# Reordering the first units of a fused attention and gated-MLP kernel, new row layouts for two inputs, and another layout of the fallback branch

## Chip, cores and metric

One core of a Trainium2 chip runs the whole program. The metric is the device time of one execution in microseconds (us), median of several executions. The engines are PE (TensorE, matmuls), DVE (VectorE), ACT (ScalarE), POOL (GpSimd) and SP, which here only issues DMAs; PSUM holds what PE writes. All executions reported here are in the undisturbed ("fast") state.

## The reference, cut to what matters

```python
mod = silu(c) @ w_mod                      # six rows of 512: sa, ca, ga, sb, cb, gb
h = layernorm(x) * (1 + ca) + sa           # x: 2048 x 512
q = (h @ wq)                               # 32 heads of 128; 8 groups share k and v
x = x + ga * (softmax(q k^T / sqrt(128)) v) @ wo
h = layernorm(x) * (1 + cb) + sb
z = gelu(h @ w_in);  z1, z2 = halves of z;  z2 = layernorm(z2)
x = x + gb * ((z1 * (w_sp @ z2 + b_sp)) @ w_out)
```

## The kernel before

The attention is a software pipeline of 128 units (8 groups of k and v, 16 query tiles each). A unit has 8 slots. In a slot the kernel first runs what is entered under `at(unit, slot, ...)`, then two score matmuls and an exp of this unit (`qk`), eight value matmuls of the unit before (`pv`), and then the `fill` matmuls, most of them query projections for later units. All engines take this order as their own program order, so an entry in the wrong slot holds up what stands behind it on its engine.

```python
def qk(u, i):
    s_ps = bank2()                                  # one of two PSUM buffers
    for h in range(2):
        nc.tensor.matmul(s_ps[...], lhsT=kT[...], rhs=qTs[b][:, :, ...])     # all four heads of qT
    nc.scalar.activation(out=pTs[u][...], in_=s_ps[...], func=Exp)

def qproj(b, heads, c0, n):                         # a list of matmuls; the fourth of a head copies it
    ...
    nc.vector.tensor_copy(out=qTs[b][...], in_=ps[0][...])                   # L894 in the profiles
```

LayerNorm of the input works in chunks of four tiles. `ln1_stats` is four pairs of statistics on VectorE (DVE), then two small GpSimd (POOL) steps for rstd, the reciprocal of the standard deviation; `ln1_norm` writes xn; `ln1_turn` transposes on TensorE (PE) and modulates on DVE; `ln1_dma` transposes by DMA instead, and `ln1_dma_mod` modulates what has landed, again on DVE.

```python
at(0, 3, lambda: ln1_turn(1, CT - 1, rest0["xn"]))          # rest of chunk 0
for k, fn in enumerate(rest_q):                             # its 16 query matmuls
    fill.setdefault((0, 5 + min(k // 5, 2)), []).append(fn)
ln1_at(1, (0, 7), (1, 3), (1, 6))                           # chunk, slots of stats, norm, turn or modulation
ln1_at(2, (1, 7), (2, 2), (3, 5))
ln1_at(3, (4, 1), (4, 5), (5, 5))
at(2, 5, lambda: nc.gpsimd.dma_start(out=wmod_b, ...))      # 2 MB
at(5, 5, lambda: nc.gpsimd.dma_start(out=win_sb, ...))      # 1.8 MB
...                                                         # v, wo, wq of the next group: slots (5,3), (6,3), (7,3)
```

Ahead of unit 0, the order of the first loads and the idle matmuls that keep PE busy while they are under way:

```python
nc.sync.dma_start(out=c_bf[:], in_=c_dram)                     # c, 1 KB
nc.sync.dma_start(out=x_sb[:, 0, :], in_=x_dram[:, 0, :])      # first tile of x
nc.sync.dma_start(out=wmod_a[:], in_=wmod_dram[:, :, 0:2 * D]) # 1 MB
...
warm(18)                                                       # matmuls on zeros
xns0 = ln1_norm(0, 1, ln1_stats(0, 1))
mod_columns(0, wmod_a, 0)                                      # 32 matmuls, need w_mod
```

At the end every engine reads a flag. If some softmax sum was out of range, a slow general path computes everything again; with these inputs it never runs.

```python
redo = nc.values_load(flag[0:1, 0:1], min_val=0, max_val=P)
with tc.If(redo != 0, preferred_fallthrough_block=False):
    general_path(...)
```

Of the kernel before, what the change touches and what calls it, by code (L numbers as in the profile page):

```python
# [15 lines left out]
P = 128  # L16
# [559 lines left out]
def kernel(  # L576
# [23 lines left out]
    REP = HQ // HKV  # L600
# [5 lines left out]
    NDT = D // P  # L606
# [3 lines left out]
    CT = 512 // P  # L610
# [12 lines left out]
    HK = SK // 2  # L623
    k_rows = A_k_cache[0, 0, 0:HK].rearrange("(p t) d -> p t d", p=P)
    v_rows = A_v_cache[0, 0, 0:HK].rearrange("(p t) d -> p t d", p=P)
    wmod_dram = w_mod.rearrange("(dt p) n -> p dt n", p=P)
    c_dram = c[0].rearrange("(j p) -> p j", p=P)
    win_dram = B_w_in.rearrange("(dt p) f -> p dt f", p=P)
    wout_dram = B_w_out.rearrange("(ft p) d -> p ft d", p=P)

# [32 lines left out]
    def bank(name):  # L663
        return psum.tile([P, 512], FP32, name=name)

    def bank2():
        return psum.tile([P, 1024], FP32, name="s_ps")
# [93 lines left out]

    def warm(n):

        w_ps = bank2()
        for k in range(n):
            nc.tensor.matmul(
                w_ps[:, 0:512].rearrange("p (r d) -> p r d", r=REP),
                lhsT=zeros[:, 0, :],
                rhs=zeros[:],
                start=True,  # L770
                stop=True,
            )
# [23 lines left out]
    def ln1_stats(j0, n):  # L796
        for j in range(j0, j0 + n):
            ln_stats(mv1, j, x_sb[:, j, :])
        return rstd_of(mv1[:, j0 : j0 + n, :], n, "ln1")

    def ln1_norm(j0, n, rstd):
        xns = []
        for j in range(j0, j0 + n):
            xn = res.tile([P, D], BF16, name="xn1", bufs=4)
            normalise(xn[:], x_sb[:, j, :], mv1[:, j, 0:1], rstd[:, j - j0 : j - j0 + 1])
            xns.append(xn)
        return xns

    def hT_of(ch):
        if ch not in hTs:  # L810
            hTs[ch] = res.tile([P, NDT, 512], BF16, name="hT", bufs=NCH)
        return hTs[ch]

    def ln1_mod(dst, src, dt):
        nc.vector.tensor_scalar(
            out=dst,
            in0=src,
            scalar1=modc[:, NDT + dt : NDT + dt + 1],
            scalar2=modc[:, dt : dt + 1],
            op0=ALU.mult,  # L820
            op1=ALU.add,
        )

    def ln1_turn(j0, n, xns, on_act=()):

        ch, c0 = j0 // CT, (j0 % CT) * P
        hT = hT_of(ch)
        for half in range(2):
            t_ps = bank("misc")[:].bitcast(BF16).rearrange("p (k q) -> p k q", k=2)
            for k in range(2):  # L830
                dt = half * 2 + k
                for jj in range(n):
                    nc.tensor.transpose(
                        t_ps[:, k, jj * P : (jj + 1) * P],
                        xns[jj][:, dt * P : (dt + 1) * P],
                        ident[:],
                    )
            for k in range(2):
                dt = half * 2 + k
                dst, src = hT[:, dt, c0 : c0 + n * P], t_ps[:, k, 0 : n * P]  # L840
                if dt in on_act:
                    nc.scalar.activation(
                        out=dst,
                        in_=src,
                        func=ACT.Identity,
                        scale=modc[:, NDT + dt : NDT + dt + 1],
                        bias=modc[:, dt : dt + 1],
                    )
                else:
                    ln1_mod(dst, src, dt)  # L850

    def ln1_dma(j0, n, xns):
        hT = hT_of(j0 // CT)
        for jj in range(n):
            nc.sync.dma_start_transpose(out=hT[:, :, jj * P : (jj + 1) * P], in_=xns[jj][:])

    def ln1_dma_mod(ch):
        for dt in range(NDT):
            ln1_mod(hTs[ch][:, dt, :], hTs[ch][:, dt, :], dt)

    warm(18)
    xns0 = ln1_norm(0, 1, ln1_stats(0, 1))
    mod_columns(0, wmod_a, 0)
    ln1_turn(0, 1, xns0, on_act=(1, 3))
    k_ps = bank("o_ps")[:].bitcast(BF16)
    for kt in range(NKT // 2):
        nc.tensor.transpose(
            k_ps[:, kt * P : (kt + 1) * P], k_nat[:, kt * P : (kt + 1) * P], ident[:]
        )
    nc.scalar.copy(out=kT0[:, 0:HK], in_=k_ps)  # L870
    warm(3)

    def qproj(b, heads, c0, n):

        g, ch = divmod(b, NCH)
        if b not in qTs:
            qTs[b] = early.tile([P, REP, 512], BF16, name="qT")
        one = n * len(heads) <= 512
        ps = {}

        def mm(hh, dt):
            if dt == 0 and (not one or hh == heads[0]):
                ps[0] = bank("misc")
            o0 = (hh - heads[0]) * n if one else 0
            nc.tensor.matmul(  # L885
                ps[0][:, o0 : o0 + n],
                lhsT=wqs[g][:, dt, hh * DH : (hh + 1) * DH],
                rhs=hTs[ch][:, dt, c0 : c0 + n],
                start=(dt == 0),
                stop=(dt == NDT - 1),  # L890
            )
            if dt == NDT - 1 and (not one or hh == heads[-1]):
                hs = heads if one else [hh]
                nc.vector.tensor_copy(  # L894
                    out=qTs[b][:, hs[0] : hs[-1] + 1, c0 : c0 + n],
                    in_=ps[0][:, 0 : len(hs) * n].rearrange("p (h q) -> p h q", q=n),
                )

        return [lambda hh=hh, dt=dt: mm(hh, dt) for hh in heads for dt in range(NDT)]
# [3 lines left out]
    rest0 = {}  # L903
# [7 lines left out]
    def at(it, slot, fn):  # L911
        later.setdefault((it, slot), []).append(fn)
# [149 lines left out]

    fill = {}
    rest_q = qproj(0, list(range(REP)), P, 512 - P)
    at(0, 3, lambda: ln1_turn(1, CT - 1, rest0["xn"]))
    for k, fn in enumerate(rest_q):
        fill.setdefault((0, 5 + min(k // 5, 2)), []).append(fn)

    def ln1_at(ch, stats, norm, turn):
        st = {}  # L1070
        at(*stats, lambda: st.update(r=ln1_stats(ch * CT, CT)))
        at(*norm, lambda: st.update(x=ln1_norm(ch * CT, CT, st["r"])))
        if ch == 1:
            at(*turn, lambda: ln1_turn(ch * CT, CT, st["x"]))
        else:
            at(norm[0], norm[1] + 1, lambda: ln1_dma(ch * CT, CT, st["x"]))
            at(*turn, lambda: ln1_dma_mod(ch))

    ln1_at(1, (0, 7), (1, 3), (1, 6))
    ln1_at(2, (1, 7), (2, 2), (3, 5))  # L1080
    ln1_at(3, (4, 1), (4, 5), (5, 5))
    rest_w = {}
    at(2, 5, lambda: nc.gpsimd.dma_start(out=wmod_b, in_=wmod_dram[:, :, 2 * D : NMOD]))
    at(5, 5, lambda: nc.gpsimd.dma_start(out=win_sb[:], in_=win_dram))
# [5 lines left out]
    def set_fill(b):  # L1090

        fs = qproj(b, list(range(REP)), 0, 512)
        for k, fn in enumerate(fs):
            it, slot = ((b - 1) * CT + k // NDT, k % NDT) if b > 1 else (2 + k // 8, k % 8)
            fill.setdefault((it, slot), []).append(fn)

    def wsp0():
# [5 lines left out]
    for g in range(1, HKV):  # L1103
        it = (g - 1) * NT + 4
# [91 lines left out]
    for it in range(NU + 6):  # L1196
        if it < NU:
            if it % CT == 0 and it // CT + 1 < NB:
                set_fill(it // CT + 1)
        elif it == NU:  # L1200
            free_a.close()
            z2p = fast.enter_context(tc.tile_pool(name="z2p", bufs=1))
            zs["z2"] = z2p.tile([P, NT, FH], BF16, name="z2")
# [154 lines left out]
    fast.close()  # L1358

    redo = nc.values_load(flag[0:1, 0:1], min_val=0, max_val=P)  # L1360
    with tc.If(redo != 0, preferred_fallthrough_block=False):
        general_path(
            tc, A_x, A_k_cache, A_v_cache, A_wq, A_wo, B_x, B_w_in, B_w_sp, B_b_sp, B_w_out,
            c, w_mod, out,
        )
# [30 lines left out]
```

## Time and profile before

| | before |
|---|---|
| median of the first 3 executions | 1338.97 us (1338.56 to 1339.24) |
| span of the profiled execution | 1337.6 us |
| PE busy, PE idle | 1305.1 us, 32.5 us |
| start of unit 0, unit 1, unit 8 | 11.77, 26.98, 92.24 us |
| a unit in steady state | 8.81 us |
| last DVE instruction to the end of the span | 8.3 us |

From unit 8 on nothing is touched by the change until the branch at the end, so three stretches can move: the 11.8 us ahead of unit 0, units 0 to 7, and the tail. The start is a chain through one load (view of the chain that ended last: start us, us, what):

```profile
1.79 5.61 DMA wmod_a<-in_w_mod_dram
7.39 0.05 issue
7.44 0.97 PE misc L782 x32
```

PE's first useful work (L782) waits for w_mod to land at 7.4 us, 5.61 us after its issue.

### The profile page before, as it was taken

To read this page: it belongs to the slowest core of one execution; us is meant where nothing else is said; L and a number is where in the kernel's file an instruction comes from. 1 tells how busy PE (TensorE), PEld (TensorE's weight loads), DVE (VectorE), ACT (ScalarE), POOL (GpSimd) and SP (SyncE) were. 2 spreads that over 40 slices of the span, in tenths; PEclk is the share of its full clock that TensorE was granted. 3 is DMA by queue.
4 is the path that set the end of the run, shared out by engine and by line. 5 is a ranking of instruction groups with operands and counts; after the bars stand their busy time and mean duration, and the time that the engine had idled before them with its cause. 6 is when DMAs were issued, how large, how long until landed. Compare 5 with 4: busy or idle time off the path is not lost.

```text
span 1337.6 us, 27647 instructions
## 1 busy us (share of the span) xinstructions
PE 1305.1 (98%) x12126; PEld 859.4 (64%) x12333; DVE 473.1 (35%) x1163; ACT 1079.3 (81%) x1060; POOL 48.6 (4%) x90
## 2 busy tenths in 40 slices
PE   7999999999999999999999999999999999999996
PEld 3666666666666666666666666666666667644444
DVE  4632222222222222222222222222222566783443
ACT  4898999999999999999999999999999999650000
POOL 1200000000000000000000000000000000020000
PEclk8999999999999999999999999999999999999999
DMA  5541022101311121012110310122101111154200
GB/s 158 131 111 17 14 63 37 21 17 33 64 21 21 33 64 21 17 36 65 17 21 17 74 30 14 21 65 36 21 13 21 25 33 33 29 123 82 55 21 27
DMA packets 146368, 57.59 MB, mean 43 GB/s; under 512 B 136544, under 2 KB 141792, under 8 KB 146240
## 3 DMA queue, kind: packets, MB, share of 16 engines
q1 hardware_dynamic: 141888, 39.29, 15.7%
q0 software_dynamic: 4208, 16.39, 4.1%
q8 instruction: 98, 1.61, 0.5%
q14 instruction: 30, 0.25, 0.1%
q10 hardware_dynamic: 144, 0.07, 0.0%
HBM read 21.37 MB, written 2.10 MB: 18 GB/s over the span
## 4 chain that ended last, share of the span: by engine, by line
PE 94%; SPq 2%; DVE 1%; issue 1%; DMA 1%; POOL 0%; ACT 0%; DVEq 0%
PE s_ps L922 35%; PE o_ps L944 35%; PE misc L885 7%; PE misc L976 6%; PE misc L1273 6%; PE s_ps L1119 2%; PE s_ps L1158 2%; SPq L1056 1%; PE o_ps L1294 1%; PE s_ps L1294 0%; DMA wmod_a<-in_w_mod_dram 0%; DMA hT<-xn 0%; DVE bnst L691 0%; DVE qT L894 0%; DMA out_dram<-yout 0%
## 5 line engine op out<-in xcount | busy, mean ns | idle before, releaser
L929 ACT ACTIVATE pT<-s_ps 128x1024 bf16<-128x1024 f32 x1024 | 1045.9, 1024 | 92.2 <-PE s_ps L922 17.1
L944 PEld LDWEIGHTS <-pT 128*128 128x128 bf16 x8192 | 549.3, 98 | 242.4 <-issue 1.8
L944 PE MATMUL o_ps<-v,pT 128*128 128x129 bf16 x8192 | 632.4, 220 | 0.4 <-DVE onorm L956 0.4
L922 PE MATMUL s_ps<-qT,kT 128*128 128x512 bf16 x2048 | 610.6, 380 | 15.5 <-DVE qT L894 4.7
L955 DVE RECIPROCAL rall<-o_ps 128x2 f32<-128x2 f32 x256 | 43.7, 171 | 742.6 <-PE o_ps L944 742.4
L922 PEld LDWEIGHTS <-kT 128*128 128x128 bf16 x2048 | 199.6, 98 | 126.2 <-DVE qT L894 4.8
L885 PE MATMUL misc<-hT,wq_g 128*128 128x512 bf16 (+2 forms) x462 | 167.7, 373 | 0.0
L976 PE MATMUL misc<-wo_g,oT 128*128 128x512 bf16 x388 | 147.0, 379 | 0.0
L956 DVE TENSOR_TENSOR onorm<-o_ps,rall 128x256 bf16<-128x256 f32 x256 | 108.7, 425 | 9.0 <-DVE rall L955 0.3
L1273 PE MATMUL misc<-wsp,z 128*128 128x512 bf16 (+2 forms) x555 | 100.5, 336 | 1.7 <-DVE gb L1288 1.1
L894 DVE CAST qT<-misc 128x512 bf16<-128x512 f32 (+1 forms) x129 | 87.2, 677 | 4.7 <-PE misc L885 4.7
L1273 PEld LDWEIGHTS <-z 128*128 128x128 bf16 x560 | 50.7, 98 | 49.5 <-issue 1.0
L989 DVE TENSOR_TENSOR xacc<-misc,xacc 128x512 f32<-128x512 f32 x112 | 76.2, 680 | 0.0
L885 PEld LDWEIGHTS <-wq_g 128*128 128x128 bf16 x528 | 51.3, 98 | 2.2 <-issue 1.1
L976 PEld LDWEIGHTS <-oT 128*128 128x128 bf16 x512 | 50.1, 98 | 0.7
L1288 DVE TENSOR_TENSOR gb<-misc,bsp_bc 128x512 bf16<-128x512 f32 (+1 forms) x28 | 18.4, 658 | 53.1 <-PE misc L1273 53.1
L712 POOL MEMSET v<- 128x128 bf16 x8 | 1.6, 204 | 715.9 <-issue 606.9
L1119 PE MATMUL s_ps<-win_sb,hT 128*128 128x448 bf16 x128 | 27.0, 352 | 0.1
L1129 ACT ACTIVATE z<-s_ps 128x896 bf16<-128x896 f32 x16 | 14.7, 917 | 14.9 <-PE s_ps L1119 14.9
L1158 PE MATMUL s_ps<-hT,win_sb 128*128 128x512 bf16 x109 | 24.3, 379 | 0.2
L1166 ACT ACTIVATE z1T<-s_ps 128x1024 bf16<-128x1024 f32 x14 | 14.3, 1024 | 10.0 <-PE s_ps L1158 9.1
L691 DVE BATCH_NORM_STATS2 bnst<-x_sb 128x6 f32<-128x512 bf16 x32 | 21.8, 682 | 0.5
(78 smaller groups left out, 281.2 us busy)
## 6 DMA issues: line engine op xcount, KB each, us to landing
v<-in_A_v_cache_dram POOLq DMA_DIRECT2D x7, 512.0 KB, 6.6
wo_g<-in_A_wo_dram POOLq DMA_DIRECT2D x7, 512.0 KB, 4.8
wq_g<-in_A_wq_dram POOLq DMA_DIRECT2D x7, 512.0 KB, 6.0
oT<-onorm SPq DMA_TRANSPOSE x128, 2.4
wsp<-in_w_mod_dram POOLq DMA_DIRECT2D x1, 2048.0 KB, 9.2
out_dram<-yout SPq DMA_DIRECT2D x15, 128.0 KB, 1.7
win_sb<-in_B_w_in_dram POOLq DMA_DIRECT2D x1, 1792.0 KB, 9.8
x_sb<-in_A_x_dram SPq DMA_DIRECT2D x3, 512.0 KB, 5.7
```

The lines of the kernel that those rows point to most:

```text
L885: nc.tensor.matmul(ps[0][:, o0 : o0 + n], lhsT=wqs[g][:, dt, hh * DH : (hh + 1) * DH], rhs=hTs[ch][:, dt, c0 : c0 + n], start=(dt == 0), s ...
L894: nc.vector.tensor_copy(out=qTs[b][:, hs[0] : hs[-1] + 1, c0 : c0 + n], in_=ps[0][:, 0 : len(hs) * n].rearrange("p (h q) -> p h q", q=n),)
L922: nc.tensor.matmul(s_ps[:, h * 512 : (h + 1) * 512].rearrange("p (r q) -> p r q", r=REP), lhsT=groups[g]["kT"][:, kt * P : (kt + 1) * P], ...
L929: nc.scalar.activation(out=pTs[u][:, 2 * i : 2 * i + 2, :], in_=s_ps[:].rearrange("p (k q) -> p k q", k=2), func=ACT.Exp, scale=inv_sqrt_dh,)
L944: nc.tensor.matmul(o_ps[:, hh % 2, 0 : DH + 1], lhsT=pTs[u][:, kt, hh * P : (hh + 1) * P], rhs=groups[g]["v1"][:, kt, 0 : DH + 1], start=( ...
L955: nc.vector.reciprocal(out=rall[:, c0 : c0 + 2], in_=o_ps[:, :, DH])
L956: nc.vector.tensor_tensor(out=onorms[u][:, hh - 1 : hh + 1, :], in0=o_ps[:, :, 0:DH], in1=rall[:, c0 : c0 + 2].unsqueeze(2).to_broadcast([ ...
L976: nc.tensor.matmul(X_ps[:], lhsT=oTs[u][:, hh, :], rhs=groups[g]["wo"][:, hh, :], start=(hh == 0), stop=(hh == REP - 1),)
L989: nc.vector.tensor_tensor(out=xaccs[j][:], in0=X_ps[:], in1=xaccs[j][:], op=ALU.add)
L1119: nc.tensor.matmul(ps[0][:, hf * 512 : hf * 512 + FC], lhsT=h2Ts[j // CT][:, dt, (j % CT) * P : (j % CT + 1) * P], rhs=win_sb[:, dt, FH + ...
L1158: nc.tensor.matmul(ps[0][:, k * 512 : (k + 1) * 512], lhsT=win_sb[:, dt, f * P : (f + 1) * P], rhs=h2Ts[2 * ch2 + k][:, dt, :], start=(dt ...
L1273: nc.tensor.matmul(g_ps[:, :n], lhsT=z2[:, st, f * P : (f + 1) * P], rhs=wsp[t][:, st, c0 : c0 + n], start=(st == 0), stop=(st == NT - 1 a ...
```

## The change

The intent: let no query copy stand behind LN statistics on DVE, let no score matmul stand behind transposes that still wait, give DMA transposes more time, keep PE busy in unit 0 with four idle matmuls (now on another PSUM bank), read c and w_mod so that a partition's rows are neighbours, and leave the branch layout to the compiler.

```diff
-    wmod_dram = w_mod.rearrange("(dt p) n -> p dt n", p=P)
-    c_dram = c[0].rearrange("(j p) -> p j", p=P)
+    wmod_dram = w_mod.rearrange("(p dt) n -> p dt n", p=P)
+    c_dram = c[0].rearrange("(p j) -> p j", p=P)
...  # in warm(n)
-        w_ps = bank2()
+        w_ps = bank("o_ps")
...
-    at(0, 3, lambda: ln1_turn(1, CT - 1, rest0["xn"]))
+    at(0, 4, lambda: ln1_turn(1, CT - 1, rest0["xn"]))
     for k, fn in enumerate(rest_q):
-        fill.setdefault((0, 5 + min(k // 5, 2)), []).append(fn)
+        fill.setdefault((0, 5 + k // 6), []).append(fn)
+    for i in range(4):
+        fill[0, i] = [lambda: warm(1)]
...
-    ln1_at(1, (0, 7), (1, 3), (1, 6))
-    ln1_at(2, (1, 7), (2, 2), (3, 5))
-    ln1_at(3, (4, 1), (4, 5), (5, 5))
+    ln1_at(1, (1, 0), (1, 5), (1, 7))
+    ln1_at(2, (2, 4), (3, 1), (4, 5))
+    ln1_at(3, (5, 1), (5, 5), (6, 6))
...  # in set_fill(b): unit and slot of the query matmul k of group of tiles b
-            it, slot = ((b - 1) * CT + k // NDT, k % NDT) if b > 1 else (2 + k // 8, k % 8)
+            it, slot = (b - 1) * CT + k // NDT, k % NDT
+            if b == 1:
+                it, slot = 2 + (2 + k) // 16, (1 + k // 2) % 8
+            elif b == 2:
+                it, slot = (5, k // 2) if k < 8 else (it, slot)
...
-    with tc.If(redo != 0, preferred_fallthrough_block=False):
+    with tc.If(redo != 0):
```

More of the change, by code (lines that the diff above doesn't have):

```diff
@@ L762, in warm @@
     def warm(n):
-        w_ps = bank2()
+        w_ps = bank("o_ps")
         for k in range(n):
             nc.tensor.matmul(
-                w_ps[:, 0:512].rearrange("p (r d) -> p r d", r=REP),
+                w_ps[:].rearrange("p (r d) -> p r d", r=REP),
                 lhsT=zeros[:, 0, :],
```

## The prediction

> **What bounds the kernel now.** I read the busy table first, then the waits of PE, then the chain of work over the first 42 us, then busy time by stretch, last the sources of the branch. The page's first part says that PE is the bound, and that little can be won:
>
> ```profile
> PE 1305.1 (98%) x12126; PEld 859.4 (64%) x12333; DVE 473.1 (35%) x1163; ACT 1079.3 (81%) x1060; POOL 48.6 (4%) x90
> ```
>
> PE is idle for 1337.6 - 1305.1 = 32.5 us in all. The attention runs in 128 units of 8 slots (score matmuls L922, exp on ACT, value matmuls L944). In the trace a unit in steady state takes 8.81 us from its first score matmul to the next unit's: 8 slots of 1.10 us, of which 0.885 is the slot's own work and 0.215 one extra matmul. The first units take 15.21, 9.64, 8.81, 10.88, 8.82, 8.81, 9.49 and 8.81 us (they start at 11.77, 26.98, 36.62, 45.43, 56.31, 65.13, 73.94, 83.43; unit 8 at 92.24). So the change can act on units 0 to 7, on the 11.77 us ahead of them, and on the tail. The waits of PE (waiter, releaser: total us, times, longest) name the holes:
>
> ```profile
> PE s_ps L922 <- DVE qT L894: 4.7, 3, 3.0
> PE misc L833 <- DVE xn L680: 1.9, 1, 1.9
> ```
>
> PE waits for the query copy (L894) and for the normalised tile (L680). The chain that ended last, early part (start, us, what), says why:
>
> ```profile
> 14.53 0.90 POOL rstd_ln L676
> 15.45 1.07 DVE xn L680 x3
> 16.52 0.05 issue
> 16.57 0.73 PE misc L833 x10
> ...
> 22.26 0.56 DVE qT L894
> 22.82 0.61 DVE bnst L691
> ...
> 26.02 0.92 DVE qT L894 x2
> 26.98 0.60 PE s_ps L922 x2
> ```
>
> The last two query copies were due at about 22.8 and stand on DVE behind four LN statistics (22.73 to 26.02), because these are put into slot (0,7) ahead of the fills. Before that, the transposes of slot (0,3) wait in PE's order for xn, so that score matmuls which need no xn wait too. Busy time by stretch (length, PE, PEld, DVE, ACT, POOL, then clock, DMA, GB/s):
>
> ```profile
> 16.00:18.00 2.00, 1.81 (x15) 1.03 (x16) 1.51 (x5) 0.17 (x1) 0.00 (x0) 0.89 1.10 348
> 18.00:20.00 2.00, 1.74 (x5) 0.56 (x4) 0.64 (x2) 1.81 (x3) 0.00 (x0) 0.50 0.76 236
> 20.00:22.00 2.00, 2.00 (x10) 1.04 (x9) 0.56 (x1) 1.20 (x2) 0.00 (x0) 0.76 0.00 0
> 24.00:26.00 2.00, 0.00 (x0) 0.00 (x0) 1.90 (x7) 0.04 (x1) 0.00 (x0) 1.00 0.00 0
> 28.00:30.00 2.00, 2.00 (x13) 1.27 (x11) 0.88 (x3) 1.60 (x2) 0.00 (x0) 0.50 0.01 4
> ```
>
> The clock falls to half after each hole; "busy" PE at 0.50 does half the work.
>
> **What the Trainium skill says.** "TensorE: Matmul & The Clock Gate", section "The HAM clock gate", has a free-running window of about 3.4 us after which an idle PE is throttled to half. The trace agrees: 0.89, 0.50, 0.76 over three times 2 us is 0.44 + 2.00 + 0.96 = 3.4 us at half. The same page, on engine queue depths, has ACT and DVE as strict FIFO; the copies behind the statistics show it. "DMA: Bandwidth & Descriptors", "Specifications", sets 512 B as the least piece for full rate. c is read in 2 B pieces, 512 of them: 1 KB lands no sooner than 128 KB.
>
> ```profile
> x_sb<-in_A_x_dram SPq DMA_DIRECT2D x1, 128.0 KB, 2.7
> c_bf<-in_c_dram SPq DMA_DIRECT2D x1, 1.0 KB, 2.8
> ```
>
> "Runtime: NRT & Kernel Launch", "Instruction fetch mechanics", says that a taken branch to a far target stalls for a fetch. The tail agrees (source view of the branch and of the end: ns min/median/max, first to last start):
>
> ```profile
> L1361 PEldq COMPARE_BRANCH  x2: 90/1858/3627, 1327.8 to 1328.1; - x2
> L1361 SPq COMPARE_BRANCH  x2: 38/48/57, 1329.0 to 1332.2; - x2
> L1391 SPq EVENT_SEMAPHORE  x14: 17/28/28, 1336.0 to 1337.6; - x14
> ```
>
> One of PE's branches takes 3.63 us, and SP does nothing visible from its last branch (1332.2) to 1336.0; the span ends 1.6 us later.
>
> **Part by part.**
>
> *c and w_mod by partition.* c becomes 128 pieces of 8 B. In the trace the 512 pieces occupy the queues from 1.88 to 3.13 us, so a quarter takes about 0.3 and 0.9 is saved there. w_mod keeps its 2 KB pieces; its gain is that c and x no longer stand ahead of it: its first piece can't start before its own issue allows (1.79 plus the 1.15 that c's first piece took from issue, 2.94 against 3.10 for the first now, up to some 0.5 later on other engines). It lands now at 1.79 + 5.6 = 7.4, and its 32 matmuls start at 7.43, the start of the path. I take **0.4 us**. wq and the first half of K queue behind it and move along.
>
> *Unit 0.* With old times: exps are 1.02 us, so the first four run 12.40 to 16.5 without a break, as slot (0,3) no longer waits. xn is ready at 16.52 as now; transposes to 17.30, score matmul of slot 4 to 17.73, exp 4 at 17.9 (now 18.90, after the delayed exp 3). hT is complete at 18.63 as now. The 16 query matmuls of 0.16 us go 6, 6, 4: to 19.2, 20.6, 21.6. The last copy (0.56) ends near 22.3, with no statistics before it, and unit 1 starts at about 22.35 in place of 26.98: **4.6 us**. The four idle matmuls cost 4 x 0.215 where PE waits for ACT anyway: nothing. They fill 0.64 of each 1.02 us, which should keep the clock up.
>
> *Unit 1.* It has little extra PE work, so it is bound by ACT, 8 x 1.02 = 8.2, plus some 0.3 for the 16 transposes moved to its last slot: 8.5 against 9.64, since the cold stretch after 27.8 is gone: **1.1 us**.
>
> *Units 2 and 3.* Now 8.81 + 10.88 = 19.69; the extra matmuls (16 query, 4 output projection) stay, so the work is 16 x 0.885 + 20 x 0.215 = 18.5. The 1.2 over it come from DVE waiting for the transposed hT of chunk 2, which competes with the 2 MB of w_mod. The modulation now comes about 11 slots after the transfer instead of 10, and both start later: I count 0.5 of wait at most, hidden by the two PSUM buffers. **1.2 us**.
>
> *Units 4 to 7.* Now 35.93 for 32 x 0.885 + 32 x 0.215 = 35.2. Unit 4 loses its fills, so it has 7.9 us of PE work under 8.2 of ACT: up to 0.25 lost. Chunk 3's transfer still meets the burst of v, win, wo and wq, which POOL issues right after the rstd of this chunk:
>
> ```profile
> DVE hT L815 <- DMA hT<-xn: 9.1, 2, 6.6
> ```
>
> The 6.6 is that wait; it cost PE only 0.4 to 0.7. From rstd to landing are 15.8 us now and the modulation gets one slot more; I expect 5.5 us of DVE wait and again some 0.5 of PE. **0**.
>
> *Branch.* On SP the eight waits for the output stores stand between its two branches, and the fetch comes after the last of them. If the default puts the fallback inline, the far jump comes at 1329.0 and its fetch (3.7) overlaps the stores (until 1331.9): about 3 us. If the automatic choice is the same as now: 0. I can't tell which; half and half, **1.5 us**.
>
> Sum: 0.4 + 4.6 + 1.1 + 1.2 + 0 = 7.3, plus 1.5 is 8.8; less 0.4 for the rivals below: 1338.97 - 8.4 = 1330.5.
>
> **Rivals.** (1) The clock falls anyway. From 14.2 to 17.6 PE has some 2.2 us of work in my schedule, against 1.8 now, which was judged idle; if that isn't enough, 3.4 us run at half and 0.5 to 1.5 come back; then about 1332. (2) DVE becomes the wait in other places: the four statistics at (2,4), 3.2 us, now delay a query copy of chunk 1, and the one at (2,7) needs its PSUM bank; or hT of chunk 3 comes so late that units 6 and 7 lose 2 us. For it speaks the 6.6 us wait, against it that PE rides 6 to 7 slots on two banks; again about 1332. (3) The start is bound by wq, which lands at 9.6 just ahead of the first query matmuls at 9.9, and not by c: only the 0.4 goes. (4) The branch is neutral: 1332; with the full overlap: 1329.
>
> **Range and chances.** Early part 6 to 8.5, branch 0 to 3.5: 1327 to 1333, widened to 1334 for clock and transfers. A gain over 2% would be 26.8 us, nearly all PE idle time; a loss of that size would need a wrong wait in every unit, and units 8 to 127 are untouched. So within 2% nearly for certain.
>
> **What would show it.** Right: unit 1 starts near 22 us and unit 8 near 85; no DVE wait of score matmuls over 1 us; clock 1.00 from 4 us on; chunk 2's hT wait gone, chunk 3's still some 5 us; c lands within some 2 us. SP's gap between its last branch and the end falls from 3.8 to under 1, or stays. Wrong: a clock of 0.50 before 35 us, a new PE wait in units 2 to 7, or unit 8 later than 87.

## The result

The changed kernel takes 1330.17 us (median of 4 executions, 1329.80 to 1332.05) against 1339.11 us (4 executions, 1338.56 to 1339.97). The ratio is 0.9936, with a 95% interval from 0.9918 to 0.9953. Ratios here are the mean time of one kernel's fast runs over that of the other's fast runs of the same rounds, so they are not quite the ratio of the medians. By the 2% rule it is "same"; the interval excludes no change.

The busy table of the changed kernel, to be set against the one in the prediction:

```profile
PE 1314.8 (99%) x12337; PEld 858.7 (65%) x12337; DVE 473.1 (36%) x1163; ACT 1077.1 (81%) x1060; POOL 48.0 (4%) x90
```

Idle PE time falls from 32.5 to 1328.3 - 1314.8 = 13.5 us. Not all of the 19 us between is gain: some matmul records were missing from the first trace (12126 matmuls there, 12337 here, of which four are new), so the difference of the spans, 9.3 us, is the figure to explain. What PE still waits for (waiter, releaser: total us, times, longest):

```profile
PE s_ps L922 <- DVE qT L894: 1.4, 2, 0.8
PE o_ps L944 <- DVE onorm L956: 1.2, 1, 1.2
...
PE misc L833 <- DVE xn L680: 0.7, 1, 0.7
```

The wait for the query copies shrinks from 4.7 to 1.4 us, with no single one over 0.8. The wait for xn shrinks from 1.9 to 0.7. The middle line, a wait of value matmuls for DVE, has grown from 0.4 to 1.2. The chain around the end of unit 0 (start us, us, what):

```profile
16.87 0.73 PE misc L833 x10
17.60 0.86 PE s_ps L922 x4
...
22.17 0.57 DVE qT L894
22.74 0.05 issue
22.78 0.60 PE s_ps L922 x2
```

No statistics stand between the last copy (22.17) and the first score matmul of unit 1 (22.78, before at 26.98). Two slots' score matmuls follow the transposes at once. Busy time by stretch (length, PE, PEld, DVE, ACT, POOL, then clock, DMA, GB/s):

```profile
16.00:18.00 2.00, 1.58 (x15) 1.06 (x16) 1.51 (x5) 0.47 (x1) 0.00 (x0) 1.00 1.13 356
18.00:20.00 2.00, 1.96 (x12) 0.94 (x10) 1.50 (x4) 1.93 (x2) 0.00 (x0) 1.00 0.82 260
...
28.00:30.00 2.00, 2.00 (x33) 1.76 (x31) 1.09 (x4) 1.95 (x3) 0.00 (x0) 1.00 0.01 4
```

The clock is 1.00 where it was 0.89, 0.50 and 0.50. Three more views answer to those of the prediction: the first loads (KB, us to landing), the DVE wait for chunk 3, and the branch with the end of the program, whose lines are now L1367 and L1397.

```profile
x_sb<-in_A_x_dram SPq DMA_DIRECT2D x1, 128.0 KB, 2.3
c_bf<-in_c_dram SPq DMA_DIRECT2D x1, 1.0 KB, 1.8
```

```profile
DVE hT L815 <- DMA hT<-xn: 7.5, 1, 7.5
```

```profile
L1367 SPq EVENT_SEMAPHORE  x8: 17/17/17, 1326.0 to 1326.5; - x8
L1367 SPq COMPARE_BRANCH  x1: 53/53/53, 1323.3 to 1323.3; - x1
L1397 SPq EVENT_SEMAPHORE  x14: 17/28/61, 1326.6 to 1328.2; - x14
```

c lands 1.0 us sooner after its issue. One of the two waits for hT is gone (9.1 us over two before), the other has grown from 6.6 to 7.5 us. On SP there is one branch in place of two, it is taken ahead of the eight waits for the stores (1323.3 against 1326.0), and the closing instructions (L1397) follow the waits within 0.1 us; before, 3.7 us lay between the last branch (1332.23) and them (1335.96).

The stretches of all profiles, in us, worked out from the starts of the score matmuls, the last DVE instruction and the end of each span:

| profile | unit 0 starts | unit 0 | unit 1 | units 2, 3 | units 4 to 7 | unit 8 to last DVE | tail |
|---|---|---|---|---|---|---|---|
| before | 11.77 | 15.21 | 9.64 | 19.69 | 35.93 | 1237.1 | 8.3 |
| changed | 12.07 | 10.71 | 8.05 | 18.47 | 36.82 | 1237.6 | 4.6 |
| changed, again (a_again) | 11.87 | 10.70 | 8.04 | 18.48 | 36.23 | 1237.8 | 4.7 |
| b_branch | 11.66 | 15.10 | 10.81 | 19.69 | 35.69 | 1237.5 | 4.8 |
| b_stats10 | 11.88 | 12.71 | 8.04 | 20.78 | 36.90 | 1237.6 | 8.0 |
| a_nobranch | 11.87 | 10.70 | 8.05 | 18.47 | 36.34 | 1237.9 | 7.4 |
| a_nowarm | 11.66 | 10.71 | 8.04 | 18.48 | 36.10 | 1237.4 | 4.6 |
| a_oldrows | 11.93 | 10.72 | 8.04 | 18.47 | 36.20 | 1238.4 | 4.6 |
| a_stats07 | 11.73 | 13.26 | 8.04 | 18.48 | 36.64 | 1237.6 | 4.6 |
| a_turn03 | 12.36 | 12.84 | 8.04 | 18.47 | 36.53 | 1239.8 | 4.6 |
| a_oldchunks | 11.88 | 10.71 | 8.04 | 20.30 | 35.51 | 1237.8 | 4.9 |
| a_winlate | 11.83 | 10.71 | 8.05 | 18.47 | 36.16 | 1237.7 | 4.7 |
| a_modlate | 11.93 | 10.71 | 8.04 | 18.48 | 35.28 | 1238.2 | 4.9 |
| a_best | 11.44 | 10.70 | 8.05 | 18.47 | 35.28 | 1237.5 | 4.7 |

From the first row to the second: +0.3, -4.5, -1.6, -1.2, +0.9, +0.5, -3.7, in sum -9.3 us, which is the difference of the spans (1328.3 - 1337.6).

### The profile page after: what moved, and what is told of

Its sections match the earlier page's. It is cut to its first block, busy times and chain, and to the rows that moved or that the text cites. A ratio compares the mean times of both kernels' runs of the same rounds, so it can differ in the third digit from the quotient of the medians.

```text
span 1328.3 us, 27856 instructions
## 1 busy us (share of the span) xinstructions
PE 1314.8 (99%) x12337; PEld 858.7 (65%) x12337; DVE 473.1 (36%) x1163; ACT 1077.1 (81%) x1060; POOL 48.0 (4%) x90
## 4 chain that ended last, share of the span: by engine, by line
PE 96%; SPq 2%; DMA 1%; DVE 1%; issue 0%; POOL 0%; DVEq 0%
PE o_ps L944 35%; PE s_ps L922 33%; PE misc L976 8%; PE misc L885 8%; PE misc L1279 6%; PE s_ps L1125 2%; PE s_ps L1164 2%; SPq L1056 1%; PE o_ps L1300 1%; PE s_ps L1300 1%; DMA wmod_a<-in_w_mod_dram 0%; DMA hT<-xn 0%; SPq L855 0%; DMA out_dram<-yout 0%; PE misc L833 0%
## 5 line engine op out<-in xcount | busy, mean ns | idle before, releaser
L976 PE MATMUL misc<-wo_g,oT 128*128 128x512 bf16 x512 | 194.0, 379 | 0.0
L885 PE MATMUL misc<-hT,wq_g 128*128 128x512 bf16 (+2 forms) x528 | 190.3, 373 | 0.0
```

Of the source, the lines that this page charges most:

```text
L885: nc.tensor.matmul(ps[0][:, o0 : o0 + n], lhsT=wqs[g][:, dt, hh * DH : (hh + 1) * DH], rhs=hTs[ch][:, dt, c0 : c0 + n], start=(dt == 0), s ...
L976: nc.tensor.matmul(X_ps[:], lhsT=oTs[u][:, hh, :], rhs=groups[g]["wo"][:, hh, :], start=(hh == 0), stop=(hh == REP - 1),)
```

## The experiments

Names with a_ start from the changed kernel, names with b_ from the kernel before. Every run gave a correct result. The kernel before ran beside each: 1339.31 us (11 executions), 1339.80 (7), 1340.64 (9). Its executions spread from 1336.45 to 1342.79 us, with mean clocks from 0.998 in the fastest to 0.993 in the slowest. A mean clock can't be read as a count of half-speed windows in the work, as it takes in the end of the span too: the profile of a_nowarm has 0.998, and all of its time at half after the start lies in its last 4.59 us, in which PE does nothing. The changed kernel has no run of its own in the second call, so a_stats07, a_turn03, a_winlate and a_modlate are compared with it across calls, and their verdicts are read from the stretches.

### The branch, both ways: b_branch and a_nobranch

```diff
-    with tc.If(redo != 0, preferred_fallthrough_block=False):
+    with tc.If(redo != 0):                      # b_branch: only this, on the kernel before
```

> The kernel before with nothing changed but the branch's layout (default). Theory (the far jump now comes ahead of the waits for the output stores, so the instruction fetch of some 3.7 us lies beside them): the stretch from the last DVE instruction to the end of the span falls from 8.3 us to about 4.6, the time from 1339.1 to about 1335.4. Rival (the layout is neutral, and the shorter tail of the changed kernel comes from something else): 1339 and a tail of 8.3 us.

> The changed kernel with the old branch layout. Theory: the tail goes back to 8.3 us, and the time to about 1333.9 (+3.7). Rival (neutral layout): 1330.2. The early part, unit 8 at 86.2 us, stays as it is in both.

b_branch took 1336.58 us (1335.96 to 1339.83), 2.7 us less than the kernel before; a_nobranch took 1333.17 us (1332.51 to 1333.88), 3.0 us more than the changed kernel. The branch and the eight waits on SP in b_branch, then the same in a_nobranch (count, ns min/median/max, first to last start):

```profile
L1361 SPq EVENT_SEMAPHORE  x8: 17/17/17, 1332.8 to 1333.3; - x8
...
L1361 SPq COMPARE_BRANCH  x1: 53/53/53, 1330.0 to 1330.0; - x1
```

```profile
L1367 SPq EVENT_SEMAPHORE  x8: 17/17/17, 1323.1 to 1325.5; - x8
...
L1367 SPq COMPARE_BRANCH  x2: 38/48/57, 1323.0 to 1325.9; - x2
```

In b_branch the branch (1330.0) comes ahead of the waits (from 1332.8); in a_nobranch a branch at 1325.9 comes after them, and the tail is 7.4 us (8.3 was expected). The layout moves the tail by about 3 us in both directions, whatever the rest of the kernel is. The theory holds and the neutral rival falls. In the profile of b_branch unit 1 takes back 1.2 of the 3.5 us that the tail gains: the clock is at half there for 6.83 us, twice as long as in the profile of the kernel before. The 2.7 us between branch and waits in the changed kernel are not a wait for the stores: in a_nobranch the first three of the eight waits are through 0.3 us after the first branch (1322.96 to 1323.23), and only the fourth stands until 1325.11. That the gap is the fetch of instructions is inferred from its position; no record names it. It is also shorter in the new layout (2.7 us against 3.1 in a_nobranch and 3.7 in the kernel before), so the overlap is not the whole gain.

### The idle matmuls: a_nowarm

```diff
-    for i in range(4):
-        fill[0, i] = [lambda: warm(1)]
```

> The changed kernel without the four idle matmuls of unit 0. Theory of the clock: the holes in unit 0 then are long enough for the clock to fall to half for one 3.41 us window in most executions, by where the window lies: 1331 to 1332.5, clocks of 0.997 to 0.998 in these. Rival (the schedule alone closes the holes, idle matmuls are not needed): 1330.2 and 0.999 in all executions, as with them; at most the one execution in four that has 0.997 with them too.

The time was 1329.68 us (6 executions, 1328.90 to 1332.04), with clocks of 0.998 and 0.999. The changed kernel has 1330.17 and 1329.81. In the profile unit 0 takes 10.71 us with and without them, and the clock stays full (columns as above):

```profile
14.00:16.00 2.00, 0.78 (x3) 0.19 (x2) 0.67 (x4) 2.00 (x3) 1.13 (x2) 1.00 1.10 349
16.00:18.00 2.00, 1.81 (x17) 1.14 (x17) 1.51 (x5) 0.40 (x2) 0.00 (x0) 1.00 1.10 349
```

The theory, a cold window in most executions, falls, and no use of the idle matmuls can be shown in the times. But that they are not needed is not shown either. The windows in which the clock is judged lie differently in each execution: the first record of full speed comes between 3.89 and 7.22 us in the 14 profiles. As they lay in this profile, the emptiest one of unit 0 has 2.18 us of PE work; the emptiest stretch of that length has less (a_nowarm first, then the changed kernel's emptiest):

```profile
12.70:16.11 3.41, 1.41 (x5) 0.38 (x4) 2.01 (x7) 3.36 (x4) 1.13 (x2) 1.00 1.13 319
```
```profile
13.50:16.91 3.41, 2.14 (x10) 0.71 (x9) 1.95 (x6) 2.97 (x4) 1.12 (x2) 1.00 1.09 337
```

Half speed followed most windows with 1.57 us or less (last section). Without the idle matmuls, windows that begin between 12.30 and 12.88 us have that little: 0.59 of 3.41 us, about one execution in six by this estimate. With them none has. Two of the six executions took over 1331 us, and two of nine of the changed kernel; that is too few to tell.

### The statistics and the transposes: a_stats07, a_turn03, b_stats10

```diff
-    ln1_at(1, (1, 0), (1, 5), (1, 7))
+    ln1_at(1, (0, 7), (1, 5), (1, 7))           # a_stats07
```
```diff
-    at(0, 4, lambda: ln1_turn(1, CT - 1, rest0["xn"]))
+    at(0, 3, lambda: ln1_turn(1, CT - 1, rest0["xn"]))      # a_turn03
```
```diff
-    ln1_at(1, (0, 7), (1, 3), (1, 6))
+    ln1_at(1, (1, 0), (1, 5), (1, 7))           # b_stats10, on the kernel before
```

> The changed kernel with only the LN statistics of chunk 1 put back to slot (0,7), ahead of the fills. Theory (the last query copies stand behind 3.2 us of statistics): unit 0 is 2.4 to 3.3 us longer (10.7 to about 13.5), and as PE then idles over 2 us, the clock falls in some executions (another 1.7 us each): 1332.5 to 1335. Rival (the gain of unit 0 came from the transposes' slot and the idle matmuls): unit 0 under 11.5 us, 1330.5.

> The changed kernel with only the transposes of unit 0 put back to slot (0,3). Theory: the fourth exp is delayed from about 15.8 to 18 us, the remaining four follow at 1.0 us, so unit 0 is about 1.0 us longer (11.7), hole of PE before it 1.7 us in place of 0.7; with the idle matmuls the clock stays at 1.00 mostly: 1331.2. Rival (PE's query matmuls bound unit 0 after the transposes, and exps have slack): unit 0 grows by under 0.5 us, 1330.4.

> The kernel before with only chunk 1 moved (statistics to (1,0), norm to (1,5), transposes to (1,7)). Theory: PE's wait of 3.0 us for the query copies and the second cold window go; unit 0 falls from 15.2 to about 12.2, unit 1 from 9.6 to 8.0 to 8.6: 1339.3 to about 1335. Rival (the wait returns in unit 1 or 2, as chunk 1's hT is late there): unit 2 over 9.5 us, 1336.5 or more.

a_stats07 took 1333.48 us (4 executions, 1331.98 to 1335.21). Unit 0 is 2.55 us longer, and PE's wait for the query copies is back, here with 3.2 us at a time:

```profile
PE s_ps L922 <- DVE qT L894: 4.0, 2, 3.2
```

a_turn03 took 1332.40 us (4 executions, 1330.74 to 1334.48), more than expected. In the profiled execution unit 0 is 2.13 us longer, as the clock fell in spite of the idle matmuls (clock is the third figure from the end):

```profile
16.00:18.00 2.00, 1.30 (x13) 1.03 (x14) 1.46 (x5) 0.00 (x0) 0.01 (x1) 0.86 1.10 350
18.00:20.00 2.00, 2.00 (x7) 0.70 (x6) 1.23 (x4) 0.94 (x1) 0.00 (x0) 0.50 0.68 210
```

The other three executions have clocks of 0.998, 0.999 and 0.999 and times of 1332.63, 1332.17 and 1330.74, so part of the cost seems to be the order itself and part the clock; the four executions don't separate them. This profile also has a second cold window near 1250 us, which no part of the edit explains and which is why its "unit 8 to last DVE" is 2 us longer.

b_stats10 took 1336.46 us (4 executions, 1334.65 to 1337.85) against 1340.64: 4.2 us less. Unit 0 falls by 2.50 us to 12.71 and unit 1 to 8.04, as expected. But units 2 to 7 are 2.1 us longer than in the kernel before, with a cold window there at 53.5 us, probably because the chunks behind were not moved along; no run separates that. So theory and rival both hold in part. The two moves in unit 0 are worth some 2.5 and 2 us, the second with a cold window in it, which makes up the 4.5 us.

### Where units 2 to 7 gain and lose: a_oldchunks, a_winlate, a_modlate

```diff
-    ln1_at(2, (2, 4), (3, 1), (4, 5))
-    ln1_at(3, (5, 1), (5, 5), (6, 6))
+    ln1_at(2, (1, 7), (2, 2), (3, 5))           # a_oldchunks; the fills of b = 1 and 2 also as before
+    ln1_at(3, (4, 1), (4, 5), (5, 5))
```
```diff
-    at(5, 5, lambda: nc.gpsimd.dma_start(out=win_sb[:], in_=win_dram))
+    at(22, 5, lambda: nc.gpsimd.dma_start(out=win_sb[:], in_=win_dram))     # a_winlate
```
```diff
-    ln1_at(3, (5, 1), (5, 5), (6, 6))
+    ln1_at(3, (5, 1), (5, 5), (7, 5))           # a_modlate
```

> The changed kernel with the schedule of chunks 2 and 3 and of the query fills of groups 1 and 2 put back. Theory (what was predicted for units 2 and 3: 1.2 us come from DVE waiting for chunk 2's hT against the w_mod load; and what the trace shows for units 4 to 7: 0.9 us lost by the move): units 2 and 3 take 19.2 to 19.8 us in place of 18.5, with a DVE wait for hT of 1.5 to 3 us there, units 4 to 7 take about 35.9 in place of 36.8; in sum 1330.2 to 1330.6, next to no difference. Rival (the old order only suffered from being late in unit 1): units 2 and 3 stay at 18.5 and the time is 1329.3.

> The changed kernel with the load of win (1.8 MB, not needed before unit 128) issued in unit 22 in place of unit 5, so that the burst of POOL loads after the rstd of chunk 3 is 1.5 MB in place of 3.3. Theory (the burst delays the transfer of chunk 3's hT, and that wait of DVE makes unit 7 long): the DVE wait for hT falls from 7.5 us to under 4, unit 7 from 10.3 to 8.8 to 9.0 us, the time by about 1 us to 1329. Rival (the transposes are slow on SP's own queue, behind each other): DVE wait stays near 7 us and unit 7 at 9.6 to 10.3.

> The changed kernel with the modulation of chunk 3 at slot (7,5) in place of (6,6). Theory (DVE stands in order before a transfer that hasn't landed): the DVE wait for hT is gone or under 1 us, unit 7 is 8.8 us, unit 8 starts 1.0 to 1.5 us earlier relative to unit 0, the time is about 1329. Rival (the wait only moves): the query matmuls of unit 8 wait for hT and unit 8 or 7 is over 9.5 us.

a_oldchunks took 1331.20 us (4 executions, 1330.95 to 1332.26), against 1329.81 for the unedited changed kernel. Units 2 and 3 take 20.30 us in place of 18.48, units 4 to 7 35.51 in place of 36.23. The two DVE waits are back, as in the kernel before:

```profile
DVE hT L815 <- DMA hT<-xn: 9.5, 2, 6.2
PE s_ps L922 <- DVE qT L894: 2.9, 3, 1.5
```

The longest wait of PE, 1.5 us at the end of unit 3, is for a query copy that stands on DVE behind the wait for chunk 2's hT, and makes up 1.5 of the 1.8 us. The rest is open: the same edit also puts the query matmuls back. So moving chunk 2 gains, moving chunk 3 loses, and the gain is the larger one: 1.8 us against 0.7, more than I had expected, so that the old order is 1.4 us slower and not about equal. The rival, units 2 and 3 at 18.5, falls.

a_winlate took 1329.40 us (4 executions, 1329.28 to 1330.72). My theory of the burst fell: with 1.8 of 3.3 MB taken out, the wait is

```profile
DVE hT L815 <- DMA hT<-xn: 6.8, 1, 6.8
```

against 7.5 and 6.9 in the two profiles of the changed kernel and 6.7 in a_nowarm, and unit 7 still takes 9.7 us. What makes these transposes slow stays open. The DMA transposes move packets of 256 B, and in the trace of the changed kernel, while the loads run (70 to 76 us), they start about as many packets as the loads do (101, 82 and 144 against 100, 83 and 145 in 2 us each, a few of 4 B counted in), where most of the loads' packets have 4 or 7 KB. But without win they start more (362, 124 and 675 against 59, 67 and 39) and still land nearly as late (the wait ends at 79.1 in place of 80.0). I have no run that tells the three other loads from the transposes' own pace.

a_modlate took 1328.99 us (4 executions, 1328.18 to 1331.07). The DVE wait for hT is gone from the profile altogether, unit 7 is 8.81 us and units 4 to 7 take 35.28, which is the PE work of 35.2 us that the prediction had counted. The theory holds for the part that matters, by the stretch and not by the time: DVE stood in order ahead of a transfer that had not landed, and everything behind it, in the end PE, waited too. The transfer is as slow as ever; it now costs nothing, because its reader comes later. The query matmuls of unit 8 do not wait.

### The start: a_oldrows

```diff
-    wmod_dram = w_mod.rearrange("(p dt) n -> p dt n", p=P)
-    c_dram = c[0].rearrange("(p j) -> p j", p=P)
+    wmod_dram = w_mod.rearrange("(dt p) n -> p dt n", p=P)
+    c_dram = c[0].rearrange("(j p) -> p j", p=P)
```

> The changed kernel with c and w_mod read in the old order of rows (both). What was predicted: 0.4 us slower than the changed kernel, as c then stands in the queue 0.9 us longer. What the trace of the changed kernel suggests: w_mod lands at 7.7 there against 7.4 before, so going back costs nothing or gains 0.3 us: unit 0 starts at about 11.8 in place of 12.1. Both are within the spread of the time; the verdict is read from the landing of w_mod and c (1.8 to 2.8 us expected for c) in the profile.

The time was 1330.04 us (6 executions, 1329.26 to 1330.46), and unit 0 starts at 11.93 us, within the 11.66 to 12.36 of the profiles with the new rows (a_best apart). The landings:

```profile
wmod_a<-in_w_mod_dram SPq DMA_DIRECT2D x1, 1024.0 KB, 5.7
...
c_bf<-in_c_dram SPq DMA_DIRECT2D x1, 1.0 KB, 2.8
```

c is back at 2.8 us, but w_mod lands 5.7 us after its issue, as with the new rows (5.6 to 6.05). The new rows speed up c by 1.0 us and do nothing for the landing of w_mod. In this profile the start doesn't even follow w_mod, which landed at 7.5 us. The chain ahead of unit 0 runs through the 18 opening idle matmuls:

```profile
1.18 6.59 PE o_ps L766 x18
7.77 0.79 PE misc L782 x32
```

These stand ahead of the w_mod matmuls on PE, and end later the later the first record of full speed comes: at 6.6 us in the profile of the kernel before (full speed from 3.89 us), at 8.2 us in that of a_turn03 (from 7.22 us), whose unit 0 therefore starts last, at 12.36. In six of the 14 profiles (a_nobranch, a_oldrows, a_stats07, a_turn03, a_oldchunks, a_winlate) the chain runs through them, in the other eight through w_mod.

### A version that beats both, and the control: a_best, a_again

```diff
-    nc.sync.dma_start(out=c_bf[:], in_=c_dram)
+    nc.scalar.dma_start(out=c_bf[:], in_=c_dram)
-    warm(18)
+    warm(13)
-    ln1_at(3, (5, 1), (5, 5), (6, 6))
+    ln1_at(3, (5, 1), (5, 5), (7, 5))
```

> The changed kernel with three edits: the modulation of chunk 3 at (7,5), c read from ACT's queue in place of SP's, and 13 opening idle matmuls in place of 18. Theory (w_mod's landing is bound by when SP issues it, not by c's pieces ahead of it): w_mod is issued 0.4 to 0.5 us earlier, lands at 6.9 to 7.1 in place of 7.3 to 7.7, unit 0 starts at 11.3 to 11.5 in place of 11.6 to 12.1; unit 7 8.8 us; time about 1328.3. Rival (the queue's bandwidth or wq bounds the start): w_mod lands at 7.3 or later and unit 0 starts at 11.7 or later; time 1329.

> The changed kernel as it is, on the same chip, as control: 1329.8 to 1330.5 with a clock of 0.998 or 0.999, one execution in four or so some 2 us longer; unit 7 9.6 to 10.3 us.

a_best took 1328.33 us (5 executions, 1327.94 to 1331.63), the changed kernel 1329.81 us (5 executions, 1329.62 to 1332.07). Four of five executions of a_best are below the fastest of the control; each kernel has one that is over 2 us slower (clocks 0.996 and 0.998). With c on another queue, SP issues w_mod earlier (timeline of SP's queue: start, us, what):

```profile
0.73 0.40 SPq L697 DMA_DIRECT2D x_sb<-in_A_x_dram  x1
1.19 0.69 SPq L698 DMA_DIRECT2D wmod_a<-in_w_mod_dram  x1
```

It is issued at 1.19 in place of 1.65 us, and unit 0 starts at 11.44 in place of 11.87. w_mod lands at 7.07 in place of 7.49, and in both profiles the chain runs through it, so the theory of the start holds there: with a_oldrows, where c's pieces take longer and w_mod lands no later, the issue sets w_mod's landing, not c's pieces. Three edits were made at once. The one in unit 7 shows in a column of its own; the two at the start are not told apart. With 18 idle matmuls, which ended between 6.6 and 8.2 us, the earlier landing would often have been no use; the 13 end at 6.8.

## Why the prediction was right

The time, 1330.17 us against 1330.5, agrees better than the steps deserve, as errors of both signs cancelled.

**Unit 0**: 4.6 us predicted, 4.50 found. The walk through the slots was right to 0.13 us, counted from the start of unit 0, and a_stats07 with a_turn03 and b_stats10 show its two causes. **Unit 1**: 1.1 predicted, 1.6 found. The cold stretch is gone, as stated. Mis-sized was "bound by ACT, 8 x 1.02 = 8.2". 1.02 us is how long the record of one exp lasts, and not the pace of exps, as records of neighbours overlap. Seven in a row take 6.52 us here, 0.90 us from start to start:

```profile
23.43 6.52 ACT L929 ACTIVATE pT<-s_ps 128x1024 bf16<-128x1024 f32 x7 [0.88 <-PE s_ps L922]
```

Seven slots of 0.88 to 0.92 us and the one with the transposes, 1.77 us, make up the 8.05. Unit 4, put at 8.2 us for the same reason, took 8.00. **Units 2 and 3**: 1.2 predicted and found. a_oldchunks shows that it is the schedule of chunk 2 with the query matmuls around it. The reason given fits in the main and not in full: of the 1.2 us, PE stood idle for 0.9 in the kernel before, waiting for a query copy behind that hT.

**Units 4 to 7**: "0" predicted, a loss of 0.2 to 0.9 found in the profiles with this schedule and both moves of unit 0 in place. The step that failed is "I expect 5.5 us of DVE wait and again some 0.5 of PE". The wait was 7.5 us (6.9 in the control), and value matmuls waited 1.2 us, a new PE wait in units 2 to 7, which the prediction had named as a sign of being wrong. The mechanism was right, as a_modlate shows; the landing came later than I took it to come, and the burst to which I put it down is not shown to be the cause.

**Start**: 0.4 predicted, nothing found. The failed step is "its gain is that c and x no longer stand ahead of it". c's pieces were done by 2.2 us in place of 3.1, yet w_mod's first piece started at 3.12 in place of 3.05 us (counted from the first record; the prediction's clock is 0.05 us ahead). w_mod waits for its own issue plus 1.3 to 1.5 us, which the 1.15 us taken from c understates. a_oldrows and a_best show both halves of this. What the prediction did not see are the opening idle matmuls, which can end after w_mod has landed.

**Branch**: 1.5 entered as the mean of two cases; the case of 3 us is the true one, with 2.7 and 3.0 us in the times. The reason given, a fetch beside the wait for the stores, fits the positions in both directions. In the profiles the tail is 3.7 us shorter, so the 1.5 was 2.2 us too low. With the 0.5 of unit 1 this made good what the start (0.7), units 4 to 7 (0.9) and the units behind (0.5) took away; that the sum came out is luck.

**Idle matmuls**: the prediction let them "keep the clock up" at no cost. They cost nothing that can be measured, and a_nowarm shows no gain either; that they keep the emptiest stretch at 2.14 us of work in place of 1.41 is read from the traces.

**Rivals**: one of four executions had a mean clock of 0.997 and took 1332.05 us. One window at half speed would cost half of 3.41 us, so this fits the first rival, but no profile of the changed kernel caught such a window. The rival's figure for the work before, 1.8 us from 14.2 to 17.6, is 1.5 in the trace; with the change it is 2.4. The second was right about chunk 3 in kind (unit 7 lost 0.8 to 1.5 us, unit 6 nothing) and wrong about the copy behind the statistics at (2,4), which shows in no unit: units 2 and 3 take their 18.5 us.

## What to carry to other kernels

In a hand-ordered pipeline, put whatever waits for a transfer or for another engine as late in its engine's order as its readers allow; a modulation that stood seven slots ahead of where its readers allow cost about 1 us, and the slow transfer behind it costs nothing once it is moved. When a load sits at the head of the critical path, look at when it is issued before shrinking what lies ahead of it in the queue. Look at the tail too: moving one branch ahead of the waits for the last stores was worth 3 us, a third of the whole gain. And the length of a record is not the pace of its engine: read the pace from one start to the next.

## What the Trainium skill lacked or had wrong

- "TensorE: Matmul & The Clock Gate", section "The HAM clock gate": the free-running window agrees; after the first warm-up, every cold stretch ahead of unit 8 in these 14 profiles is 3.41 us or twice that. What it lacks is how much work keeps a window warm. In the first 16 windows of each profile, full speed followed all windows with at least 1.88 us of PE busy time unless the clock was already at half, and half speed followed 7 of the 8 with 1.57 us or less (0.80 and 1.43 in the kernel before, 1.01 and 1.44 in b_stats10, 1.16 and 1.37 in b_branch, 1.57 in a_turn03; one of 1.42 in a_stats07 stayed at full speed). Between 1.57 and 1.88 none was seen.
- "Runtime: NRT & Kernel Launch", section "Instruction fetch mechanics": a far taken branch does stall, but the page gives no time. PE's branch took 3.3 to 3.9 us in the 14 profiles. On SP, 2.7 us lay between branch and next record in the changed kernel and 3.7 us in the kernel before. Nor does it say that waits for stores placed behind the branch lie beside this stall (b_branch).
- None of the pages named in this document says what DMA transposes take beside other loads: 12.7 us in the median from issue to landing for those of chunk 3, against 2.4 us for those of the attention outputs over the run.
